# Four buffers for two exps, early tiles laid elsewhere, and a new order for two pairs of products and a few late jobs, in a fused attention and MLP kernel

## The chip, the cores and the metric

The kernel runs on one core of one Trainium2 chip. The metric is the device time of one execution in microseconds.

Engines in the profile: PE is the matmul engine (TensorE), PEld its weight loads, DVE is VectorE, ACT is ScalarE, POOL is GpSimd, SP issues most DMAs (25 of the 26 groups of DMA issues in the profile of the kernel before, ACT the other). "L1193" is a line of the kernel file; since the change adds lines, the same instruction has another line number after it.

## The reference

One input x of 2048 tokens by 1024 is layer-normalized and goes into two branches whose outputs are added to x.

```
xn = layernorm(x)
A: q, k, v = xn @ wq, xn @ wk, xn @ wv          # 32 heads of 32, four segments of 512 tokens
   per segment: p = softmax(q k^T * scale + causal mask);  a_dot = p v
                a_mem = phi(q) M / (phi(q) z)   # phi(t) = t + 1 if t > 0 else exp(t)
                o = g * a_mem + (1 - g) * a_dot
                M += phi(k)^T v;  z += sum phi(k)
   A = o @ wo
B: h = layernorm(xn);  u = gelu(h^T w1 + b1);  y = u w2 + b2;  B = y^T
out = x + A + B
```

## The kernel before

The kernel runs in three stages: the norm with the first ("early") 512 columns of w1; the MLP's products; attention in 32 units (four heads of one segment each).

**MLP products.** Each pair of 128-column blocks of w1 (and later of w2) is multiplied by a scheme of seven products instead of eight: products 1, 6, 5, 7, 2, 4, 3 of 8 (w1) or 14 (w2) matmuls of 128x512. They accumulate in three PSUM banks X, Y, Z; between two products on the same bank, DVE or ACT takes a partial sum out. Their operands are sums of w1 blocks ("sum") and differences of blocks of h or of the hidden layer g ("hT", "gT"; one of the gT is written over a g block), made on DVE.

```python
class _Pair:
    ACC = {1: "X", 2: "X", 6: "Y", 7: "Y", 4: "Y", 5: "Z", 3: "Z"}
...
# products():
order = [(0, 1), (1, 1), (0, 2), (1, 2)] + [(0, p) for p in (6, 5, 7, 4, 3)] + [(1, p) for p in (6, 5, 7, 4, 3)]
order += [(i, p) for i in range(2, n1 + self.N_W2) for p in self.ORDER]
...
# after1(), what follows product p of pair i:
elif p == 6:
    self.add_bank(pair, "Y", t2, t1)
    while self.later:                 # the g differences of pairs done, all at once
        self.later.popleft()()
...
elif p == 3:
    ...
    self.later.append(lambda: self.g_diff(j))        # four subtractions each
    if i == 0:
        self.later.append(lambda: self.g_diff(0))
        self.later.append(lambda: self.g_diff(1))
```

**Early tiles.** The input xin, a junk tile, a warm-up tile and the early w1 block lie where the hidden blocks g11, gT2, gT1, g12, g21, gT4, g22 come later, seven blocks of 14336 bytes a partition. In the kernel before, xin lies first and the early w1 block is under gT1 and g12. A gelu that writes g12 must therefore wait until the last matmul has read the early w1 block: in the trace one gelu runs at 31.45 us and the next seven from 34.47 us, with the early matmuls from 6.64 to 34.43 us.

**Attention.** For unit u, while its logits are exponentiated, the projections of unit u+2 run as fill-in jobs of 8 matmuls. The end of the q job puts three instructions on ACT and the end of the k job one on DVE and one on ACT:

```python
def q_job(self, u):
    def end(b):
        ... "act": qT[k] = copy of the bank
        if u >= N_GRP:
            ... "act": etmp[0] = exp(qT[k])          # writes etmp[0]
def k_job(self, u):
    def end(b):
        ... "dve": kT[k] = copy of the bank
        if u // N_GRP < N_SEG - 1:
            ... "act": etmp[1] = exp(kT[k])
def phi(self, dst, R_dst, src, R_src, k):           # k = 0 for q, 1 for k
    ... "dve": mtmp[k] = min(etmp[k], 1)            # reads etmp[k]
    ... "dve": dst = max(src + 1, mtmp[k])
def logits(self, u, step):                          # into banks 0 to 3
    ...
    ... "act": pT = exp(scale * banks 0..3)          # frees the banks for the next logits
```

Within unit u the program calls `logits(u, 0)`, `weigh(u-1, ..)`, `phi_k(u+1)`, `logits(u, 1)`, `combine(u-1)`, `phi_q(u+1)`, in even units `logits(u, 2)`, with fill-in matmuls between them. `combine` is about 3 us of DVE (476.53 to 479.37 us in one unit of the kernel before). The fill-in jobs also hold the products with wo of the segment before ("wo jobs"), each followed by an addition into fin on DVE.

The softmax here doesn't subtract the row's maximum and nothing guards it: scores larger than these inputs give would overflow.

Of the kernel before, what the change touches and what calls it, by code (L numbers as in the profile page):

```python
# [19 lines left out]
P = 128  # L20
# [364 lines left out]
class _Kernel:  # L385
# [33 lines left out]
    def alloc(self):  # L419
        k = _Walk(self.mem, 0, self.G_AT)  # L420

        def one(name, shape, dtype):
            t, (r,) = k.take(name, shape, dtype)
            setattr(self, name, t)
            setattr(self, "R_" + name, r)

        one("ident", [P, P], BF16)
        self.brow1, self.R_brow1 = k.take("brow1", [P, 32], BF16, 5)
        self.brow2, self.R_brow2 = k.take("brow2", [P, 32], BF16, 5)
        one("bcol", [P, 2, 32], BF16)  # L430
        one("b1c", [P, N_FCH], F32)
        one("b2c", [P, N_TCH], F32)
        one("beta", [P, N_HEAD], BF16)
        one("gcol", [P, N_HEAD], F32)
        one("gate", [P, N_GRP, 2, 4], F32)
        one("eps8", [P, 2, 4], F32)
        self.ln_st, self.R_st = k.take("ln_st", [P, N_TCH, 12], F32, N_TCH)
        self.ln_mv = k.take("ln_mv", [P, N_TCH, 2], F32)[0]
        self.ln_rs, self.R_rs = k.take("ln_rs", [P, N_TCH, 2], F32, N_TCH)
        self.R_rs0 = Res("rs0")  # L440
        one("expo", [P, N_TCH], F32)
        self.ln_sm = k.take("ln_sm", [P, N_TCH, 1], F32)[0]
        self.srec, self.R_srec = k.take("srec", [P, 2, 32], F32, 2)
        self.R_out = [Res(f"out{c}") for c in range(N_TCH)]

        e = _Walk(self.mem, self.G_AT, self.B_AT)
        self.xin, self.R_xin = e.take("xin", [P, N_TCH, D_MODEL], BF16, N_TCH)
        one_e = e.take("junk", [P, D_MODEL], BF16)
        self.junk, (self.R_junk,) = one_e
        self.warm, (self.R_warm,) = e.take("warm", [P, 512], BF16)  # L450
        self.w1early, self.R_w1e = e.take("w1early", [P, N_TCH, 512], BF16, N_TCH)

        b = _Walk(self.mem, self.B_AT + 6400, self.SB_END - self.SB_BASE)
        self.h = [[None, None], [None, None]]
        R = [[None, None], [None, None]]
        for k2 in range(2):
            both, res = b.take(f"h{k2}", [P, 2, 8, 512], F16, 1)
            self.mem.live.pop()
            for d in range(2):
                self.h[k2][d] = both[:, d]  # L460
                R[k2][d] = [Res(f"h{k2}{d}_{i}") for i in range(8)]
                lo = self.SB_BASE + b.at - 16384 + 8192 * d
                self.mem.live.append((lo, lo + 8192, R[k2][d]))
            setattr(self, f"h_{k2}", both)
        self.R_h = R
        self.hT, self.R_hT = [], []
        for i in (0, 1, 3):
            t, (r,) = b.take(f"hT{i}", [P, 8, 512], F16)
            self.hT.append(t[:])
            self.R_hT.append([r])  # L470
        self.hT.insert(2, self.h[0][1])
        self.R_hT.insert(2, R[0][1])
        self.w1s, self.R_w1s = [], []
        for i in range(2):
            t, (r,) = b.take(f"w1s{i}", [P, N_TCH, 256], BF16)
            self.w1s.append(t)
            self.R_w1s.append(r)
        self.s1, self.R_s1 = [], []
        for i in range(2):
            t, r = b.take(f"sum1_{i}", [P, 4, 8, P], F16, 4)  # L480
            self.s1.append(t)
            self.R_s1.append(r)
        self.tmp, self.R_tmp = [], []
        for i in range(6):
            t, (r,) = b.take(f"part{i}", [P, 512], F32)
            self.tmp.append(t)
            self.R_tmp.append(r)
# [214 lines left out]
    def products(self):  # L702
        fw = self.fw
        g = _Walk(self.mem, self.G_AT, self.B_AT)
        for b in range(8):
            if b == 0:
                self.alloc_hidden(g)
            self.gelu(b // 2, b % 2, self.bank(b), self.R_bank[b])
        self.h_diff((1, 2))
        self.pairs = {}  # L710
        n1 = self.N_W1
        order = [(0, 1), (1, 1), (0, 2), (1, 2)] + [(0, p) for p in (6, 5, 7, 4, 3)] + [(1, p) for p in (6, 5, 7, 4, 3)]
        order += [(i, p) for i in range(2, n1 + self.N_W2) for p in self.ORDER]
        self.later = deque()
        for i, p in order:
            if i not in self.pairs:
                self.begin_pair(i)
            pair = self.pairs[i]
            self.product(pair, p)
            pair.done.add(p)  # L720
            (self.after1 if i < n1 else self.after2)(pair, p)
# [22 lines left out]
    def h_diff(self, which):  # L744
        self.differences(self.h, self.R_h, self.hT, self.R_hT, which)

    def g_diff(self, j):
        self.differences([[t[:, j] for t in row] for row in self.gB], [[[r[j]] for r in row] for row in self.R_gB],
                         [t[:, j] for t in self.gT], [[r[j]] for r in self.R_gT], (1, 2, 3, 4))

    def begin_pair(self, i):
        n1 = self.N_W1
# [38 lines left out]
    def after1(self, pair, p):  # L791
# [13 lines left out]
                self.alloc_w2_first()  # L805
        elif p == 6:
            self.add_bank(pair, "Y", t2, t1)
            while self.later:
                self.later.popleft()()
        elif p == 7:  # L810
            self.add_bank(pair, "Y", t3, t1)
        elif p == 2:
            self.gelu(2 * j, 0, self.bank(pair.bank["X"]), self.R_bank[pair.bank["X"]])
        elif p == 4:
            if i + 2 < self.N_W1:
                self.w1_ring.ensure(i + 2)
            self.add_bank(pair, "Y", t1, t1)
            self.gelu(2 * j + 1, 0, self.tmp[t1][:], self.R_tmp[t1])
        elif p == 3:
            self.add_bank(pair, "Z", t2, t2)  # L820
            self.gelu(2 * j, 1, self.tmp[t2][:], self.R_tmp[t2])
            self.later.append(lambda: self.g_diff(j))
            if i == 0:
                self.later.append(lambda: self.g_diff(0))
                self.later.append(lambda: self.g_diff(1))
        if p in (5, 7) and {5, 7} <= d:
            self.add_bank(pair, "Z", t3, t3)
            self.gelu(2 * j + 1, 1, self.tmp[t3][:], self.R_tmp[t3])
# [11 lines left out]
                self.pair_sums(i + 1, (4,))  # L840
                self.alloc_w2_rest()
        elif i:
            if p == 7:
                self.pair_sums(i + 1, (1,))
            elif p == 2 and i > 1:
                self.pair_sums(i + 1, (2,))
            elif p == 4:
                self.pair_sums(i + 1, (2, 3) if i == 1 else (3,))
            elif p == 3:
                self.pair_sums(i + 1, (4,))  # L850
        elif p == 7:
            self.pair_sums(1, (1, 2))
        elif p == 3:
            self.pair_sums(1, (3, 4))

    W2_AT = (0, 14336)
    S2_AT = (38912 + 256, 53248 + 256)
# [132 lines left out]
    def before_attention(self, p):  # L990
# [23 lines left out]
        elif p == 5:  # L1014
# [4 lines left out]
                fw.op("pool", lambda e: e.memset(self.vA[k][:], 1.0), writes=self.R_vA[k])  # L1019
            self.qT, self.R_qT = many("qT", 3, [P, SEG_L], BF16)  # L1020
            self.kT, self.R_kT = many("kT", 3, [P, SEG_L], BF16)
            self.etmp, self.R_etmp = many("etmp", 2, [P, SEG_L], BF16)
            self.mtmp, self.R_mtmp = many("mtmp", 2, [P, SEG_L], BF16)
        elif p == 7:
            self.pqT, self.R_pqT = many("pqT", 3, [P, SEG_L], BF16)
# [32 lines left out]
                      reads=[self.R_diag], writes=[self.R_diag])  # L1058


    def phi(self, dst, R_dst, src, R_src, k):

        fw = self.fw
        et, mt = self.etmp[k], self.mtmp[k]
        fw.op("dve", lambda e: e.tensor_scalar(mt[:], et[:], 1.0, None, op0=ALU.min),  # L1065
              reads=[self.R_etmp[k]], writes=[self.R_mtmp[k]])
        fw.op("dve", lambda e: e.scalar_tensor_tensor(dst, src, 1.0, mt[:], op0=ALU.add, op1=ALU.max),  # L1067
              reads=[R_src, self.R_mtmp[k]], writes=[R_dst])

    def phi_q(self, u):  # L1070
        if N_GRP <= u < N_UNIT:
            k = u % 3
            self.phi(self.pqT[k][:], self.R_pqT[k], self.qT[k][:], self.R_qT[k], 0)

    def phi_k(self, u):
        if u // N_GRP < N_SEG - 1:
            k = u % 3
            self.phi(self.mtmp[1][:], self.R_mtmp[1], self.kT[k][:], self.R_kT[k], 1)

    def k_transpose(self, u):  # L1080
        if u // N_GRP < N_SEG - 1:
# [3 lines left out]
    def q_job(self, u):  # L1085
        def end(b):
# [1 line left out]
            fw.op("act", lambda e: e.activation(self.qT[k][:], self.bank(b), ACT.Copy),  # L1088
                  reads=[self.R_bank[b]], writes=[self.R_qT[k]])
            if u >= N_GRP:  # L1090
                fw.op("act", lambda e: e.activation(self.etmp[0][:], self.qT[k][:], ACT.Exp),  # L1091
                      reads=[self.R_qT[k]], writes=[self.R_etmp[0]])
        return self.proj_job(self.wq_ring, u, end)

    def k_job(self, u):
        def end(b):
# [1 line left out]
            fw.op("dve", lambda e: e.tensor_copy(self.kT[k][:], self.bank(b)),  # L1098
                  reads=[self.R_bank[b]], writes=[self.R_kT[k]])
            if u // N_GRP < N_SEG - 1:  # L1100
                fw.op("act", lambda e: e.activation(self.etmp[1][:], self.kT[k][:], ACT.Exp),
                      reads=[self.R_kT[k]], writes=[self.R_etmp[1]])
        return self.proj_job(self.wk_ring, u, end)

    def proj_job(self, ring, u, end):
# [208 lines left out]
    def attention(self):  # L1314
        self.jobs, self.turn = deque(), 0
        self.wo_plan = {}
        for s in range(N_SEG - 1):
            at = [N_GRP * s + 10 + n for n in range(8)] if s < 2 else [26, 27, 28, 29, 30, 30, 31, 31]
            for n, u in enumerate(at):
                self.wo_plan.setdefault(u, []).append((4 * s + n // 2, n % 2))  # L1320
        self.jobs.extend([self.q_job(0), self.k_job(0)] + [self.v_job(0, c) for c in range(4)])
# [59 lines left out]
    def tail(self):  # L1381
# [35 lines left out]
        product(4, 0, 7)  # L1417
        self.o_transpose(u, 4)
        product(3, 6, 7)
        for n in range(5):  # L1420
            product(n, 7, 8)
        for n in range(5, 7):
            product(n, 0, 8)
        product(7, 0, 8, ((0, 256), (256, 384), (384, 512)))


# [26 lines left out]
```

## Time and profile before

Three runs: 686.55, 684.60 and 682.38 us, median 684.6. The page of the profile, parts of its head (engine, busy us and share of the span, instructions):

```profile
span 682.0 us, 11096 instructions
PE 652.6 (96%) x4622; PEld 301.3 (44%) x4622; DVE 421.7 (62%) x789; ACT 282.8 (41%) x305; POOL 145.3 (21%) x181
```

TensorE is the limit, and only its idle stretches can be won without taking work away. The view of waits of PE (waiter, what it waited for: us in total, times, longest):

```profile
PE ps_all L198 <- ACT pT L1193: 16.2, 17, 1.8
PE ps_all L198 <- DVE part L688: 3.2, 2, 2.4
PE ps_all L198 <- DVE fin L1141: 1.9, 2, 1.3
```

The 3.2 us behind "part" are in the first two w1 pairs. The timeline of PE there (start us, us, engine, line, op, out<-in, tile, form, count; in brackets the idle time before it and what ended it):

```profile
34.27 1.89 PE L198 MATMUL ps_all<-h,w1s 128*128 128x512 f16 x8
36.46 1.89 PE L198 MATMUL ps_all<-h,w1s 128*128 128x512 f16 x8 [0.30 <-ACT g L740]
39.17 3.63 PE L198 MATMUL ps_all<-h,w1s 128*128 128x512 f16 x16 [0.83 <-ACT part L693]
48.76 1.90 PE L198 MATMUL ps_all<-hT,w1s 128*128 128x512 f16 x8 [0.78 <-DVE part L688]
...
59.96 3.54 PE L198 MATMUL ps_all<-hT,w1s 128*128 128x512 f16 x8 [2.39 <-DVE part L688]
63.34 1.89 PE L198 MATMUL ps_all<-h,sum 128*128 128x512 f16 x8
65.06 1.89 PE L198 MATMUL ps_all<-h,w1s 128*128 128x512 f16 x8
```

Two pairs are 14 products. A product of 8 matmuls that waits for nothing starts 1.73 us after the one before it, so 14 take 24.2 us; here 34.27 to 65.06 is 30.8 us. What the 2.39 us wait is made of shows in the timeline of DVE: twelve subtractions of gT and g, then the addition that the product at 59.96 waits for.

```profile
54.83 0.41 DVE L662 TENSOR_TENSOR gT<-g,g 128x512 f16<-128x512 f16 x1
...
58.89 0.42 DVE L662 TENSOR_TENSOR gT<-g,gT 128x512 f16<-128x512 f16 x1
59.22 1.41 DVE L688 TENSOR_TENSOR part<-ps_all,part 128x512 f32<-128x512 f32 x2
```

And 8 matmuls take 3.54 us after that gap instead of 1.89. The view of stretches of two us (stretch, its length, then busy us and count for PE, PEld, DVE, ACT and POOL; the granted clock, the DMA share, GB/s):

```profile
58.00:60.00 2.00, 0.04 (x1) 0.04 (x2) 1.93 (x6) 0.00 (x0) 0.00 (x0) 0.97 0.00 0
60.00:62.00 2.00, 2.00 (x5) 0.70 (x6) 1.23 (x2) 0.72 (x1) 0.00 (x0) 0.50 0.00 0
62.00:64.00 2.00, 2.00 (x8) 0.76 (x7) 0.46 (x1) 0.00 (x0) 0.00 (x0) 0.67 0.00 0
```

From 60 to 62 us PE is busy for 2.00 of 2.00 us, but with 5 matmuls at clock 0.50 (the view counts a matmul in every stretch that it touches): it is at half clock. So this stretch is 100% busy at half the rate, which only the count of matmuls and the clock column show.

The 16.2 us behind pT are in attention. One instance, the end of an even unit, in the timelines of ACT, then DVE, then PE:

```profile
478.54 0.60 ACT L1088 ACTIVATE qT<-ps_all 128x512 bf16<-128x512 f32 x1 [0.31 <-PE ps_all L198]
480.10 0.63 ACT L1091 ACTIVATE etmp<-qT 128x512 bf16<-128x512 bf16 x1 [0.96 <-DVE mtmp L1065]
480.64 1.86 ACT L1193 ACTIVATE pT<-ps_all 128x2048 bf16<-128x2048 f32 x1
...
479.29 0.72 DVE L1065 TENSOR_SCALAR mtmp<-etmp 128x512 bf16<-128x512 bf16 x1
...
482.55 0.40 PE L198 MATMUL ps_all<-qT,kT 32*128 32x512 bf16 x4 [1.02 <-ACT pT L1193]
```

The exp of q (L1091) can't overwrite etmp before phi of the unit before has read it (L1065, ended 480.01). The pT eviction stands behind it in ACT's queue, though its logits had been there since about 478.8, and the next logits on PE wait for that. ACT did not take the eviction out of turn: the trace has 0.96 us of ACT idle with the pT eviction ready behind. The view of waits of ACT in attention (370 to 682 us):

```profile
ACT etmp L1091 <- DVE mtmp L1065: 23.5, 16, 2.1
ACT etmp L1101 <- DVE kT L1098: 10.5, 14, 2.0
```

### The profile page before, as it was taken

The page shows a single profiled execution, that of the slowest core. Times are in us where ns is not written, and L with a number is a line of the kernel's source. Part 1 is how long each engine was busy: PE and PEld are TensorE (multiplying, and loading weights), DVE is VectorE, ACT ScalarE, POOL GpSimd, SP SyncE. Part 2 cuts the span into 40 slices and gives each one's busy share as a digit, 9 for nine tenths or more (in the row PEclk, how much of TensorE's full clock was granted, in tenths as well). Part 3 has the DMA queues.
Part 4 walks back from the last instruction along what each step waited for, and adds up shares of the span by engine and source line. Part 5 has one row for each costly group of instructions (what it writes and reads, how often), then busy time and mean ns, then how long its engine had stood idle before and what let it go on. Part 6 is the DMA issues. An engine that isn't in the chain of part 4 may idle for free.

```text
span 682.0 us, 11096 instructions
## 1 busy us (share of the span) xinstructions
PE 652.6 (96%) x4622; PEld 301.3 (44%) x4622; DVE 421.7 (62%) x789; ACT 282.8 (41%) x305; POOL 145.3 (21%) x181
## 2 busy tenths in 40 slices
PE   8988999999999999999999999998998899999888
PEld 3433444444444444444444444444444344444434
DVE  7857665656652445324531554697777897776685
ACT  7442132232300000000105878856666667666660
POOL 3500000000020122211240333322332232322240
PEclk9998999999999999999999999999999999999999
DMA  9704223242637654556385685665537755434314
GB/s 319 176 0 122 65 80 105 62 124 62 176 118 201 161 160 132 135 171 169 87 276 132 148 155 116 122 132 136 125 91 157 143 118 113 114 88 94 79 47 132
DMA packets 187242, 87.65 MB, mean 129 GB/s; under 512 B 116024, under 2 KB 174392, under 8 KB 187192
## 3 DMA queue, kind: packets, MB, share of 16 engines
q1 hardware_dynamic: 187048, 86.91, 51.0%
q8 instruction: 36, 0.59, 0.4%
q14 instruction: 14, 0.11, 0.1%
q10 hardware_dynamic: 144, 0.03, 0.0%
HBM read 67.13 MB, written 8.39 MB: 111 GB/s over the span
## 4 chain that ended last, share of the span: by engine, by line
PE 76%; DVE 13%; ACT 7%; DMA 3%; issue 1%; SPq 0%; ACTq 0%
PE ps_all L198 76%; ACT pT L1193 4%; DVE prod L1280 3%; DMA xs<-in_A_x_dram 2%; DVE mtmp L1065 2%; DVE o_s L1284 1%; ACT etmp L1091 1%; DVE ost L1243 1%; DVE mtmp L1067 1%; DVE fin L1141 1%; DVE srec L1278 1%; ACT g L740 1%; DMA xin<-in_A_x_dram 1%; DVE xs L981 1%; DVE srec L1279 0%
## 5 line engine op out<-in xcount | busy, mean ns | idle before, releaser
L1193 ACT ACTIVATE pT<-ps_all 128x2048 bf16<-128x2048 f32 x80 | 149.7, 1871 | 30.8 <-PE ps_all L198 30.7
L1197 POOL TENSOR_SCALAR_AFFINE_SELECT pT<-pT 128x512 bf16<-128x512 bf16 x128 | 92.2, 738 | 221.8 <-ACT pT L1193 221.8
L688 DVE TENSOR_TENSOR part<-ps_all,part 128x512 f32<-128x512 f32 x76 | 53.7, 706 | 124.8 <-PE ps_all L198 124.4
L921 POOL TENSOR_TENSOR part<-part,stg 128x512 f32<-128x512 f32 x24 | 33.0, 1404 | 269.3 <-DVE part L688 269.3
L693 ACT ACTIVATE part<-ps_all 128x512 f32<-128x512 f32 x20 | 11.9, 602 | 147.9 <-PE ps_all L198 147.9
L740 ACT ACTIVATE g<-part,b1c 128x512 f16<-128x512 f32 x36 | 26.0, 722 | 104.1 <-DVE part L688 104.1
L198 PE MATMUL ps_all<-wo,oT 128*128 128x512 bf16 (+2 forms) x272 | 64.7, 367 | 2.4 <-DVE fin L1141 1.9
L198 PE MATMUL ps_all<-wv,xnT 128*128 128x512 bf16 x256 | 66.6, 379 | 0.0
L198 PE MATMUL ps_all<-xnT,wq 128*128 128x512 bf16 x256 | 65.1, 380 | 0.0
L1243 DVE CAST ost<-ps_all 128x396 bf16<-128x396 f32 (+2 forms) x96 | 42.8, 473 | 34.6 <-PE ps_all L198 33.8
L198 PE MATMUL ps_all<-xnT,wk 128*128 128x512 bf16 x256 | 61.6, 380 | 0.0
L198 PE MATMUL ps_all<-g,w2s 128*128 128x512 f16 x224 | 51.0, 379 | 0.0
L198 PE MATMUL ps_all<-g,sum 128*128 128x512 f16 x224 | 51.0, 379 | 0.0
L198 PEld LDWEIGHTS ps_all<-vA,pT 128*128 128x128 bf16 x1280 | 42.2, 96 | 19.8 <-DVE ost L1243 10.2
L198 PE MATMUL ps_all<-gT,sum 128*128 128x512 f16 x224 | 49.7, 379 | 0.0
L198 PE MATMUL ps_all<-qT,kT 32*128 32x384 bf16 (+3 forms) x512 | 31.7, 301 | 16.5 <-ACT pT L1193 16.2
L198 PE MATMUL ps_all<-vA,pT 128*128 128x33 bf16 x1280 | 45.1, 178 | 1.6 <-DVE ost L1243 1.5
L198 PE MATMUL ps_all<-h,w1s 128*128 128x512 f16 x192 | 45.2, 379 | 1.1 <-ACT part L693 0.8
L198 PE MATMUL ps_all<-h,sum 128*128 128x512 f16 x192 | 45.4, 379 | 0.0
L198 PE MATMUL ps_all<-hT,sum 128*128 128x512 f16 x192 | 43.4, 379 | 0.0
L198 PEld LDWEIGHTS ps_all<-xnT,wk 128*128 128x128 bf16 x256 | 23.8, 98 | 29.8 <-issue 3.2
L198 PEld LDWEIGHTS ps_all<-wo,oT 128*128 128x128 bf16 x272 | 23.0, 97 | 28.6 <-issue 5.4
(98 smaller groups left out, 817.3 us busy)
## 6 DMA issues: line engine op xcount, KB each, us to landing
w2s<-in_B_w_dram SPq DMA_DIRECT2D x8, 1792.0 KB, 8.5
w1s<-in_B_w_dram SPq DMA_DIRECT2D x12, 1024.0 KB, 5.7
wq<-in_A_wq_dram SPq DMA_DIRECT2D x32, 256.0 KB, 3.4
wk<-in_A_wk_dram SPq DMA_DIRECT2D x32, 256.0 KB, 3.9
stg<-in_A_x_dram SPq DMA_DIRECT2D x16, 256.0 KB, 2.9
xs<-in_A_x_dram SPq DMA_DIRECT2D x16, 256.0 KB, 4.1
out_dram<-stg SPq DMA_DIRECT2D x16, 256.0 KB, 2.9
fin<-out_dram SPq DMA_DIRECT2D x16, 256.0 KB, 2.9
```

What stands on the lines that cost most here:

```text
L198: ins = self.nc.tensor.matmul(*args, **kwargs)
L688: self.fw.op("dve", lambda e: e.tensor_tensor(self.tmp[dst][:], self.bank(b), self.tmp[src][:], op=ALU.add), reads=[self.R_bank[b], self.R ...
L693: self.fw.op("act", lambda e: e.activation(self.tmp[dst][:], self.bank(b), ACT.Copy), reads=[self.R_bank[b]], writes=[self.R_tmp[dst]])
L740: self.fw.op("act", lambda e: e.activation(self.gB[f % 2][half][:, f // 2, :], src, ACT.Gelu_apprx_tanh, bias=self.b1c[:, f:f + 1], scale= ...
L921: fw.op("pool", lambda e: e.tensor_tensor(self.tmp[t][:], self.tmp[t][:], self.stg[k][:, 512 * half:512 * half + 512], op=ALU.add), reads= ...
L981: self.fw.op("dve", lambda e: e.tensor_scalar(x[:], x[:], self.ln_mv[:, c, 0:1], self.ln_rs[:, c, 0:1], op0=ALU.subtract, op1=ALU.mult), r ...
L1065: fw.op("dve", lambda e: e.tensor_scalar(mt[:], et[:], 1.0, None, op0=ALU.min), reads=[self.R_etmp[k]], writes=[self.R_mtmp[k]])
L1067: fw.op("dve", lambda e: e.scalar_tensor_tensor(dst, src, 1.0, mt[:], op0=ALU.add, op1=ALU.max), reads=[R_src, self.R_mtmp[k]], writes=[R_ ...
L1193: fw.op("act", lambda e: e.activation(dst, src, ACT.Exp, scale=SCALE), reads=self.R_bank[0:4], writes=[R[v % 2][kb] for v, kb, _ in blocks ...
L1197: fw.op("pool", lambda e: e.affine_select(d, d, pattern=[[0, 4], [1, P]], compare_op=ALU.is_ge, fill=0.0, base=0, channel_multiplier=-1), ...
L1243: fw.op("dve", lambda e: e.tensor_copy(dst, src), reads=[self.R_bank[b]], writes=[self.R_ost[o][part]])
L1280: fw.op("dve", lambda e: e.tensor_tensor(self.prod[:], ost[:, :, 0:D_HEAD], rec.unsqueeze(2).to_broadcast([P, 32, D_HEAD]), op=ALU.mult), ...
```

## The change

It is meant to take four kinds of idle time from PE: (1) lay the early tiles so that the first gelus need not wait for the last early matmul; (2) weave the products of the first two w1 pairs, and hand out the g subtractions one per product from pair 2 on; (3) give exp of q and exp of k a buffer for each parity of the unit; (4) at the end, move one wo job from unit 26 to unit 31 and one product of the tail ahead of the last pieces of the others.

```diff
-        self.xin, self.R_xin = e.take("xin", [P, N_TCH, D_MODEL], BF16, N_TCH)
         one_e = e.take("junk", [P, D_MODEL], BF16)
         self.warm, (self.R_warm,) = e.take("warm", [P, 512], BF16)
+        e.at = self.G_AT + 14336
         self.w1early, self.R_w1e = e.take("w1early", [P, N_TCH, 512], BF16, N_TCH)
+        e.at = self.G_AT + 3 * 14336
+        self.xin, self.R_xin = e.take("xin", [P, N_TCH, D_MODEL], BF16, N_TCH)
...
-        order = [(0, 1), (1, 1), (0, 2), (1, 2)] + [(0, p) for p in (6, 5, 7, 4, 3)] + [(1, p) for p in (6, 5, 7, 4, 3)]
+        order = [(0, 1), (1, 1), (0, 2), (1, 2), (0, 6), (0, 5), (0, 7), (1, 6), (0, 4), (1, 5), (1, 7), (0, 3), (1, 4), (1, 3)]
...
         elif p == 6:
             self.add_bank(pair, "Y", t2, t1)
-            while self.later:
-                self.later.popleft()()
...
-            self.later.append(lambda: self.g_diff(j))
-            if i == 0:
-                self.later.append(lambda: self.g_diff(0))
-                self.later.append(lambda: self.g_diff(1))
+            for jj in ((j, 0, 1) if i == 0 else (j,)):
+                for k in range(1, 5):
+                    self.later.append(lambda jj=jj, k=k: self.g_diff(jj, (k,)))
...   (the sums of w1 blocks for pairs 1 and 2 move to other products of pair 0)
+        if self.later and i > 1 and not (last and p == 3):
+            self.later.popleft()()
...
-            self.etmp, self.R_etmp = many("etmp", 2, [P, SEG_L], BF16)
+            self.etmp, self.R_etmp = many("etmp", 4, [P, SEG_L], BF16)
...   (exp of q of unit u: etmp[2 * (u % 2)]; exp of k: etmp[2 * (u % 2) + 1]; phi reads the same)
-            at = ... [26, 27, 28, 29, 30, 30, 31, 31]
+            at = ... [27, 28, 29, 30, 30, 31, 31, 31]
...   (tail)
-        for n in range(5):
+        product(5, 0, 7)
+        for n in range(6):
             product(n, 7, 8)
-        for n in range(5, 7):
-            product(n, 0, 8)
+        product(6, 0, 8)
```

More of the change, by code (lines that the diff above doesn't have):

```diff
@@ L745, in h_diff, with g_diff @@
         self.differences(self.h, self.R_h, self.hT, self.R_hT, which)
-    def g_diff(self, j):
+    def g_diff(self, j, which):
         self.differences([[t[:, j] for t in row] for row in self.gB], [[[r[j]] for r in row] for row in self.R_gB],
-                         [t[:, j] for t in self.gT], [[r[j]] for r in self.R_gT], (1, 2, 3, 4))
+                         [t[:, j] for t in self.gT], [[r[j]] for r in self.R_gT], which)
     def begin_pair(self, i):
@@ L842, in after1 @@
         elif i:
-            if p == 7:
+            if p == 7 and i > 1:
                 self.pair_sums(i + 1, (1,))
@@ L850, in after1 @@
                 self.pair_sums(i + 1, (4,))
-        elif p == 7:
+        elif p == 2:
             self.pair_sums(1, (1, 2))
+        elif p == 6:
+            self.pair_sums(1, (3,))
+        elif p == 5:
+            self.pair_sums(1, (4,))
         elif p == 3:
-            self.pair_sums(1, (3, 4))
+            self.pair_sums(2, (1,))
+        if self.later and i > 1 and not (last and p == 3):
+            self.later.popleft()()
     W2_AT = (0, 14336)
@@ L1058, in before_attention, with phi @@
                       reads=[self.R_diag], writes=[self.R_diag])
-    def phi(self, dst, R_dst, src, R_src, k):
+    def phi(self, dst, R_dst, src, R_src, k, u):
         fw = self.fw
-        et, mt = self.etmp[k], self.mtmp[k]
+        et, R_et, mt = self.etmp[2 * (u % 2) + k], self.R_etmp[2 * (u % 2) + k], self.mtmp[k]
         fw.op("dve", lambda e: e.tensor_scalar(mt[:], et[:], 1.0, None, op0=ALU.min),
-              reads=[self.R_etmp[k]], writes=[self.R_mtmp[k]])
+              reads=[R_et], writes=[self.R_mtmp[k]])
         fw.op("dve", lambda e: e.scalar_tensor_tensor(dst, src, 1.0, mt[:], op0=ALU.add, op1=ALU.max),
@@ L1072, in phi_q @@
             k = u % 3
-            self.phi(self.pqT[k][:], self.R_pqT[k], self.qT[k][:], self.R_qT[k], 0)
+            self.phi(self.pqT[k][:], self.R_pqT[k], self.qT[k][:], self.R_qT[k], 0, u)
     def phi_k(self, u):
@@ L1077, in phi_k @@
             k = u % 3
-            self.phi(self.mtmp[1][:], self.R_mtmp[1], self.kT[k][:], self.R_kT[k], 1)
+            self.phi(self.mtmp[1][:], self.R_mtmp[1], self.kT[k][:], self.R_kT[k], 1, u)
     def k_transpose(self, u):
@@ L1090, in end @@
             if u >= N_GRP:
-                fw.op("act", lambda e: e.activation(self.etmp[0][:], self.qT[k][:], ACT.Exp),
-                      reads=[self.R_qT[k]], writes=[self.R_etmp[0]])
+                fw.op("act", lambda e: e.activation(self.etmp[2 * (u % 2)][:], self.qT[k][:], ACT.Exp),
+                      reads=[self.R_qT[k]], writes=[self.R_etmp[2 * (u % 2)]])
         return self.proj_job(self.wq_ring, u, end)
@@ L1100, in end @@
             if u // N_GRP < N_SEG - 1:
-                fw.op("act", lambda e: e.activation(self.etmp[1][:], self.kT[k][:], ACT.Exp),
-                      reads=[self.R_kT[k]], writes=[self.R_etmp[1]])
+                fw.op("act", lambda e: e.activation(self.etmp[2 * (u % 2) + 1][:], self.kT[k][:], ACT.Exp),
+                      reads=[self.R_kT[k]], writes=[self.R_etmp[2 * (u % 2) + 1]])
         return self.proj_job(self.wk_ring, u, end)
@@ L1317, in attention @@
         for s in range(N_SEG - 1):
-            at = [N_GRP * s + 10 + n for n in range(8)] if s < 2 else [26, 27, 28, 29, 30, 30, 31, 31]
+            at = [N_GRP * s + 10 + n for n in range(8)] if s < 2 else [27, 28, 29, 30, 30, 31, 31, 31]
             for n, u in enumerate(at):
```

## The prediction

> **What bounds it now.** TensorE: the page has it busy 652.6 of 682.0 us (96%), and "in step" the matmuls start about 0.216 us apart (128x512; 590 in 129.15 us in the chain of waits). Only its idle stretches can be won. The view of waits (PE) adds them up: 16.2 us behind pT evictions (ACT, 17 times), 3.2 behind part additions (DVE), 1.9 behind fin additions.
>
> **1. First two w1 pairs (timeline, 34 to 65 us).** 14 products of 8 matmuls should take 14 x 1.728 = 24.2 us; they take 30.8 (34.27 to 65.06): 6.6 us lost. Idle: 0.30 and 0.83 us (gelu of early bank 1 started only at 34.47, after the last early matmul, because g12 overlays w1early), 0.78 (product (0,4) behind the addition of (0,7)), 2.39 (product (1,4) behind an addition queued after twelve gT/g subtractions of 0.42 us); each also costs about 0.15 us of refill. After the 2.39 us gap the granted clock was 0.50 for 2 us and 0.67 for the next 2, costing another 1.65 us. [...]
> The change lays g11/g12/g21/g22 over tiles whose readers are done, so gelus start bank by bank from 31.5; weaves the pairs so that a product on another bank lies between an addition and the next product on its bank; defers the subtractions to pairs 2 onward, one per product (56 x 0.42 us, DVE is only 58% busy there). Stepping through the new order with these durations I find no wait: **-6.4 us**.
>
> **2. Exp of q in attention.** ACT waits 23.5 us (16 times) to write etmp for q, because phi of the previous unit has not read it on a backlogged DVE; the next pT eviction, and then TensorE, wait behind it. Nine waits of TensorE show it (441 to 642 us: 1.28, 1.78, 1.02, 1.08, 1.78, 1.78, 1.02, 1.40, 1.70), 12.8 us, plus 0.15 each. With four buffers the exp waits for nothing but qT. What remains is ACT's qT copy, exp, pT in a row (0.6+0.6+1.8 us), about 0.25 us behind TensorE, as at 604.7 us (a pair of units there: 18.6 us, 18.5 busy). Exp of k still waits for the kT copy on DVE, so the small waits (0.22, one of 1.01 on ost) stay. DVE: busy about 16.7 of 19.4 us a pair, not the limit. **-11.9 us**.
>
> **3. End.** product(5,0..7) before the last oT covers the 0.47 us wait: **-0.6**. Moving one wo job from unit 26 to 31 fills unit 31, but the fin addition behind combine may hold the tail (0.69 us now): **+0.2**, at most 0.5 either way.
>
> Sum -18.7 us, all on the critical path: **about 666 us (662 to 670.5)**. Faster by over 2%: 0.90; within 2%: 0.095; slower: 0.005.
>
> **Right if:** (1,3) ends near 58.5 and the whole w2 part shifts by 6.4 us, granted clock 1.00 from 50 to 70; the ACT wait "etmp of q behind mtmp" vanishes and PE's wait for pT falls from 16.2 to 3-5 us; pairs of units 8 to 23 take 19.2-19.5 us instead of 20.3-21.2; TensorE busy time falls only by 1-2 us, its share to 98%.
>
> **Wrong if:** the faster pace makes DVE the limit (waits on ost, kT, mtmp grow), xs loads or transposes land late, or the deferred subtractions delay an addition in pairs 2 to 6; then attention keeps 4 to 6 us.

The clock of 0.50 and its 1.65 us are read from the profile of before, and the sum is -6.4 - 11.9 - 0.6 + 0.2 = -18.7 us. The 0.15 us of refill is that of the front: products start 2.19 us apart with a wait of 0.30 us between them (34.27 and 36.46) and 2.71 us apart with 0.83 us (36.46 and 39.17), where 1.73 us do without a wait. For the nine waits in attention it is the author's estimate, carried over from there, and was not shown: at the wait of 1.02 us above, the logits start 2.04 us after the wo matmuls before them (480.51 and 482.55), in the kernel after 1.12 us (472.25 and 473.37), so 0.92 us less.

## The result, and the profile after

After: 666.27, 667.62, 665.92 and 666.37 us, median 666.3. Before, on the same chip: median 685.6 of four runs. The ratio is 0.9729 (95% interval 0.9691 to 0.9768), 2.7% faster. All ratios here are the mean time of one kernel's fast runs over the mean of the other's in the same rounds, so not quite the ratio of the medians.

The page of the kernel after, the same lines:

```profile
span 664.5 us, 11075 instructions
PE 650.2 (98%) x4622; PEld 301.1 (45%) x4622; DVE 421.5 (63%) x789; ACT 282.9 (43%) x305; POOL 145.7 (22%) x181
```

No engine does less work: the counts of matmuls and of DVE and ACT instructions are the same. PE's busy time falls by 2.4 us; most of that is the half-clock stretch of before. Its waits:

```profile
PE ps_all L198 <- ACT pT L1198: 4.3, 11, 0.8
PE ps_all L198 <- DVE h L628: 1.8, 1, 1.8
PE ps_all L198 <- DVE ost L1248: 1.6, 3, 1.0
PE ps_all L198 <- DVE fin L1146: 1.3, 1, 1.3
```

The front, PE's timeline: no wait left, and 24.17 us from 35.26 to 59.43 for the 14 products.

```profile
35.26 7.07 PE L198 MATMUL ps_all<-h,w1s 128*128 128x512 f16 x32
...
57.70 1.89 PE L198 MATMUL ps_all<-h,sum 128*128 128x512 f16 x8
59.43 1.89 PE L198 MATMUL ps_all<-h,w1s 128*128 128x512 f16 x8
```

And the stretch that was at half clock:

```profile
60.00:62.00 2.00, 2.00 (x11) 0.88 (x9) 1.33 (x3) 1.32 (x2) 0.00 (x0) 1.00 1.16 330
```

In attention, the end of the same even unit, ACT then PE: the exp of q follows qT at once, and the logits come without a wait.

```profile
470.29 0.60 ACT L1093 ACTIVATE qT<-ps_all 128x512 bf16<-128x512 f32 x1 [0.32 <-PE ps_all L198]
470.92 0.63 ACT L1096 ACTIVATE etmp<-qT 128x512 bf16<-128x512 bf16 x1
471.46 1.86 ACT L1198 ACTIVATE pT<-ps_all 128x2048 bf16<-128x2048 f32 x1
...
473.37 0.40 PE L198 MATMUL ps_all<-qT,kT 32*128 32x512 bf16 x4
```

The waits of ACT in attention (370 to 665 us) have no line for exp of q any more, and a longer one for exp of k:

```profile
ACT etmp L1106 <- DVE kT L1103: 23.1, 16, 2.7
```

Of the 23.5 us that ACT spent waiting for phi of q, 12.6 (23.1 less 10.5) turned up again as a wait for the kT copy. The rest, 10.9 us, is close to what attention got shorter by; the traces do not tie the two together wait by wait. PE's waits show no loss from the longer wait of exp of k: those for pT are 4.3 us with it, against 16.2 before.

**Where the time went, stretch by stretch.** The starts of the first early matmul, the first w1 matmul and the first logits of units 0, 8, 25 and 29 in PE's timeline divide each span (the last column ends with the span):

```
kernel             first early  early part  w1 and w2, to unit 0  units 0-8  8-25    25-29  29 to end
before             6.64         27.63       334.99                62.14      173.32  36.91  40.37
after              7.45         27.81       328.18                61.53      163.94  34.14  41.45
exp buffers only   6.92         27.63       335.13                61.53      163.27  35.68  40.64
without them       6.83         29.29       328.24                61.53      173.33  35.36  41.52
exp of q only      6.97         27.70       328.23                62.52      163.24  34.14  41.60
old layout         7.07         29.31       329.61                62.18      163.23  34.14  41.46
old order          6.89         27.63       330.30                61.54      163.28  34.13  41.53
not deferred       6.45         29.32       332.15                61.92      163.25  34.14  41.47
after again        7.78         30.32       328.25                61.15      163.23  34.13  41.44
wo at 26           7.08         29.26       328.23                62.12      163.27  35.69  40.45
three wo in 30     6.74         27.77       328.24                62.11      163.25  34.14  41.15
combine last       7.14         27.62       329.54                62.11      163.25  34.13  40.01
fin first          6.84         28.13       328.26                61.15      163.27  34.13  39.72
12 warm-ups        7.01         27.83       328.19                62.11      163.27  34.13  39.76
```

Two things can be read here. First, a stretch that an edit does not touch repeats within 0.15 us from kernel to kernel from the third column on (units 0 to 8, which wait for a load of xs, within 1.4 us; "combine last" lost 0.2 and 0.8 us in two waits in the products that no other run shows; "after" lost 0.5 us in units 8 to 25, a wait behind a kT copy that had itself stood behind an xs load, DVE idle 1.18 us). So a stretch tells fractions of a microsecond that the times, which spread by 0.5 to 6 us within one kernel, do not. Second, what else varies lies mostly in the head: the first early matmul starts between 6.45 and 7.78 us, and the early part takes 27.6 to 28.1 or 29.3 to 30.3 us. (Each kernel has one profile; the spread of the other runs was not traced.)

The long early parts run at half the rate too. In the five kernels with 29.3 us or more, the first 8 to 13 early matmuls start 0.43 us apart instead of 0.216, which is 1.7 to 2.7 us more; in the other nine at most one gap is longer than 0.25 us. "After again", in stretches of one us (4 matmuls in each, then 6):

```profile
9.00:10.00 1.00, 1.00 (x4) 0.43 (x3) 1.00 (x4) 0.97 (x3) 0.40 (x1) 1.00 1.04 381
12.00:13.00 1.00, 1.00 (x4) 0.44 (x3) 0.86 (x4) 0.91 (x2) 0.55 (x1) 1.00 1.06 388
13.00:14.00 1.00, 1.00 (x6) 0.37 (x4) 1.00 (x3) 0.99 (x2) 0.40 (x1) 1.00 1.05 383
```

The clock column says 1.00 here. Of the five kernels it says 0.50 only in "old layout" (8 to 10 us, with 3 to 4 matmuls in each us); in the other four the half rate is read from the distance of the matmuls alone. It is not the edits that decide it: the same kernel has it in "after again" (30.32 us) and not in "after" (27.81 us).

The change from before to after is then +0.8 and +0.2 us in the head (chance), -6.8 in the products, -0.6 in units 0 to 8, -9.4 in units 8 to 25, and -1.7 in the rest, together -17.5 us, the difference of the spans.

### The profile page after: what moved, and what is told of

Read it like the earlier page. It is cut to its first block, busy times and chain, and to the rows that moved or that the text cites. A ratio compares the mean times of both kernels' runs of the same rounds, so it can differ in the third digit from the quotient of the medians.

```text
span 664.5 us, 11075 instructions
## 1 busy us (share of the span) xinstructions
PE 650.2 (98%) x4622; PEld 301.1 (45%) x4622; DVE 421.5 (63%) x789; ACT 282.9 (43%) x305; POOL 145.7 (22%) x181
## 4 chain that ended last, share of the span: by engine, by line
PE 81%; ACT 8%; DVE 7%; DMA 2%; issue 1%; SPq 0%; DVEq 0%
PE ps_all L198 81%; ACT pT L1198 6%; DMA xs<-in_A_x_dram 1%; DVE prod L1285 1%; ACT etmp L1096 1%; ACT qT L1093 1%; DVE mtmp L1070 1%; DMA xin<-in_A_x_dram 1%; DVE kT L1103 1%; DVE pqT L1072 1%; DVE o_s L1289 1%; ACT etmp L1106 1%; DVE fin L1406 1%; DVE ost L1248 0%; DVE xs L986 0%
```

## The experiments

Theory: the waits of PE add up. Front: layout about 1.4 us, order about 2, deferral the rest with the clock dip; attention: exp of q behind phi of q. Rivals: one part of the front carries it all; in attention exp of k matters as much, or the gain needs the other parts of the change.

**Exp buffers only** (kernel before, with the four buffers).

```diff
-            self.etmp, self.R_etmp = many("etmp", 2, [P, SEG_L], BF16)
+            self.etmp, self.R_etmp = many("etmp", 4, [P, SEG_L], BF16)
     (and the indices of the change)
```

> The kernel before with nothing changed but four exp buffers. My theory (exp of q waited for phi of the unit before, and the pT eviction and TensorE behind it): 11 to 12 us shorter than before, so ratio about 0.983; TensorE's waits for pT fall from 16.2 to about 4.5 us, ACT's waits of etmp of q for mtmp from 23.5 to 0, while the front still shows its 2.4 us gap. Rival (the gain in attention needs the earlier or smoother start, or the moved wo jobs): under 8 us.

Measured: median 673.9 us, ratio 0.9845 (0.9814 to 0.9875), 10.6 us by the ratio; the span fell by 11.2 us. The stretches from unit 8 on, where all nine long waits of before lie, give 11.0 us; units 0 to 8 give 0.6 more, within their scatter. PE's wait for pT:

```profile
PE ps_all L198 <- ACT pT L1193: 4.0, 10, 0.8
```

ACT's wait of etmp of q is gone, that of etmp of k went to 23.6 us (from 370 us on). The front is that of before, with 2.40 us of wait and granted clock 0.50 after it. The rival falls: the gain needs nothing else of the change.

**Without them** (kernel after, with two buffers).

```diff
-            self.etmp, self.R_etmp = many("etmp", 4, [P, SEG_L], BF16)
+            self.etmp, self.R_etmp = many("etmp", 2, [P, SEG_L], BF16)
     (and the indices of before)
```

> The kernel after with the exp buffers back to two. My theory: 11 to 12 us longer than after, so about 677.5 us, ratio to before about 0.990; nine waits of TensorE for pT of 1.0 to 1.8 us come back; products unchanged (no wait from 35 to 65 us). Rival (the wo move or the tail order had taken part of it): less than 9 us back.

Measured: median 679.6 us, ratio 0.9924. All nine waits came back with their sizes (1.02 to 1.79 us), and PE's wait for pT with them:

```profile
PE ps_all L198 <- ACT pT L1198: 16.2, 18, 1.8
```

In the stretches, units 8 to 25 take 173.33 against 163.25 us and units 25 to 29 take 1.22 us more: 11.3 us. The time is 12.4 us above that of "exp of q only" of the same rounds; the profile has 1.6 us more in its early part, the half rate at the head (matmuls 0.43 us apart).

**Exp of q only** (kernel after, with two buffers for q and one for k).

```diff
-        et, R_et, mt = self.etmp[2 * (u % 2) + k], self.R_etmp[2 * (u % 2) + k], self.mtmp[k]
+        j = 1 if k else 2 * (u % 2)
+        et, R_et, mt = self.etmp[j], self.R_etmp[j], self.mtmp[k]
...     (exp of k writes etmp[1] in every unit; etmp has 3 tiles)
```

> The kernel after with two buffers for exp of q and a single one for exp of k. My theory: only the q buffer was waited for (no wait of etmp of k for mtmp stands in the profile before), so the time of after, 666 us, within 1 us, ratio about 0.973. Rival (both exps block ACT, each half of the gain): 670 to 672 us, and a wait of etmp of k for mtmp shows up.

Measured: median 667.1 us, ratio 0.9747; units 8 to 25 take 163.24 us, as in after. No wait of exp of k for a phi appears. The fourth buffer is worth nothing here: phi of k runs early in the unit, long before the next exp of k (in before, which also has one buffer for k, phi's read of it ended at 475.55 and 487.67 us, and the next exp of k began at 482.40 and 493.17 us).

**Old layout** (kernel after, with the early tiles where they were).

```diff
+        self.xin, self.R_xin = e.take("xin", ...)      # first again
-        e.at = self.G_AT + 14336
-        e.at = self.G_AT + 3 * 14336
-        self.xin, self.R_xin = e.take("xin", ...)
```

> The kernel after with the early tiles laid as before (g12 over w1early). My theory: early bank 1's gelu waits again for the last early matmul, TensorE loses 0.46 and 0.98 us before products 2 and 3 of the w1 part, 1.4 us in all: about 667.8 us. Rival (the layout is what frees the whole front): 4 to 6 us longer, with waits also after 42 us.

Measured: 668.3 us. The waits of 0.30 us behind gelu and 0.82 us behind the copy are back, none later; the stretch of the products takes 329.61 instead of 328.2 us, 1.4 us, as expected.

**Old order** (kernel after, first two pairs in the old order with their sums at the old places, subtractions deferred).

```diff
-        order = [(0, 1), ..., (0, 6), (0, 5), (0, 7), (1, 6), (0, 4), (1, 5), (1, 7), (0, 3), (1, 4), (1, 3)]
+        order = [(0, 1), ...] + [(0, p) for p in (6, 5, 7, 4, 3)] + [(1, p) for p in (6, 5, 7, 4, 3)]
...   (the sums of w1 blocks for pairs 1 and 2 at their places of before)
```

> The kernel after with the first two w1 pairs in the old order and their weight sums at the old places; the g subtractions stay deferred to pair 2 and come one by one. My theory (12 queued subtractions made the 2.4 us gap and, with it, the clock dip; the order only hides one addition per pair): two waits of about 0.8 us, before (0,4) and before (1,4), no dip of the granted clock, so 1.9 us longer than after, about 668.3 us. Rival (the weave is what removes the gap): a wait over 2 us before (1,4) and the clock dip come back, 4 to 5 us longer.

Measured: 668.6 us. Two waits and no dip (granted clock 1.00 from 44 to 62 us); the stretch is 2.1 us longer than in after. PE's timeline:

```profile
47.56 1.90 PE L198 MATMUL ps_all<-hT,w1s 128*128 128x512 f16 x8 [0.79 <-DVE part L690]
...
57.16 1.90 PE L198 MATMUL ps_all<-hT,w1s 128*128 128x512 f16 x8 [0.79 <-DVE part L690]
```

The deferral alone thus turned the 2.39 us wait into one of 0.79; the weave takes away the two that are left.

**Not deferred** (kernel after, woven, subtractions all at once behind product 6).

```diff
         elif p == 6:
             self.add_bank(pair, "Y", t2, t1)
+            while self.later:
+                self.later.popleft()()
...
-        if self.later and i > 1 and not (last and p == 3):
-            self.later.popleft()()
```

> The kernel after, woven, but the g subtractions again all at once behind the addition after product 6 (now 16 of them at pair 2, as product (0,3) comes after (1,6)). My theory: the block of about 6 us on DVE only moves to pair 2; (2,4) then waits about 2.1 us for the addition of (2,7), and the granted clock dips or not: 2.3 to 4 us longer than after, 668.6 to 670.3 us. Rival (the weave alone was enough): within 1 us of after, no wait.

Measured: 669.1 us; the stretch is 4.0 us longer. PE's timeline and the stretches:

```profile
70.81 3.09 PE L198 MATMUL ps_all<-hT,w1s 128*128 128x512 f16 x8 [2.07 <-DVE part L690]
```

```profile
70.00:72.00 2.00, 1.19 (x5) 0.47 (x6) 1.97 (x4) 0.48 (x1) 0.00 (x0) 0.84 0.00 0
72.00:74.00 2.00, 2.00 (x6) 0.75 (x5) 0.83 (x3) 0.81 (x2) 0.00 (x0) 0.50 0.00 0
74.00:76.00 2.00, 2.00 (x9) 0.82 (x8) 1.23 (x2) 0.72 (x1) 0.00 (x0) 0.80 0.25 70
```

The block of subtractions has only moved to pair 2, sixteen of them now, and makes the same gap there with the same dip: 2.1 us of wait and about 1.9 of refill and half clock. Undoing layout, order or deferral alone costs 1.4, 2.1 and 4.0 us, 7.5 in sum, where all together gave 6.8: they overlap, most likely because the wait of product (1,4) is counted twice: it was one wait of 2.39 us before, and shows as 0.79 in "old order" and as 2.07 (there of product (2,4)) in this one. The 4.0 us are those of the profiled run, with its half clock; that may not come in every execution (point 4 below).

**Wo jobs at 26** (kernel after, wo jobs where they were), with **after again** in the same rounds.

```diff
-            at = ... [27, 28, 29, 30, 30, 31, 31, 31]
+            at = ... [26, 27, 28, 29, 30, 30, 31, 31]
```

> The kernel after, unchanged, for comparison on the same chip as the next three: 666 us (665 to 668). From the first logits on (363 us in the first profile) its stretches should repeat within 0.3 us, except for the one wait of 0.5 us behind a kT copy, which the other runs did not show; what varies should be the head, before the first early matmul and in the granted clock just after it.

> The kernel after with the wo jobs of the last segment back at 26, 27, 28, 29, 30, 30, 31, 31. The prediction gave the move +0.2 us; the two profiles suggest that it is worth about 0.4 us instead, since the wait of 0.69 us at the tail (fin addition behind combine) is gone and a wait of 0.27 for ost has come. So 0.3 to 0.6 us longer than after, from the stretches of the profile; the times alone may not tell it.

Measured: after again 665.5 us (ratio 0.9749), wo at 26 667.4 us (664.9 to 671.0; its ratio 0.9771, told "unclear"). The times can't tell them apart. The stretches from unit 25 on can: 76.14 us (35.69 + 40.45) against 75.57, so the move is worth 0.57 us (of which 0.18 is a wait for oT that only "wo at 26" shows). The tail's wait of 0.68 us is back:

```profile
648.84 1.47 PE L198 MATMUL ps_all<-wo,oT 128*128 128x512 bf16 x6 [0.68 <-DVE fin L1146]
```

With the wo jobs and the tail's order both old ("exp buffers only") the same stretches take 76.32 us, 0.18 us more, hardly above their scatter. From the last transposes to the end of the span the order of the tail shows better: 9.69 and 9.70 us in the two kernels with the old order, 9.42 to 9.45 in the twelve with the new one. It is worth 0.26 us. After again also had an early part of 30.32 us in its profile with nothing changed.

**Three wo jobs in unit 30**, then **combine last**, **fin first** and **12 warm-up matmuls**: what is left after the change is mostly one wait of 1.27 us at the start of unit 31, behind a fin addition that stands on DVE behind combine(29) and phi_q(31). These four build on each other; the diffs are against after.

```diff
-            at = ... [27, 28, 29, 30, 30, 31, 31, 31]
+            at = ... [27, 28, 29, 30, 30, 30, 31, 31]       # three wo in 30
...
-            if u:
+            if u and u < N_UNIT - 1:                        # combine last ("fin first": u < N_UNIT - 2)
                 self.combine(u - 1)
-            self.phi_q(u + 1)
+            if u != N_UNIT - 2:                             # fin first
+                self.phi_q(u + 1)
...
                 self.dense(cuts[3])
+                if u == N_UNIT - 2:                         # fin first
+                    self.combine(u - 1)
                 self.logits(u, 2)
             self.dense(100)
+            if u == N_UNIT - 2:                             # fin first
+                self.phi_q(u + 1)
+        self.combine(N_UNIT - 2)                            # combine last
         self.tail()
...
-    N_WARM = 10
+    N_WARM = 12                                             # 12 warm-up matmuls
```

> The kernel after with the moved wo jobs at units 27, 28, 29, 30, 30, 30, 31, 31 rather than 27, 28, 29, 30, 30, 31, 31, 31: one job more in unit 30, whose first job then ends ahead of the combine on DVE. If the waits of unit 30 (0.58 for pT, 1.27 behind the fin addition queued after combine and phi) come from too few matmuls between the logits, both nearly go, 1.8 us; the wait of 0.7 us at the tail behind the last fin addition comes back. Net 0.5 to 1.2 us shorter than after.

Measured: 665.4 us; from unit 29 to the end 41.15 us against 41.45, 0.3 us, less than expected: of the two waits in unit 30 the one of 0.58 us went, but 1.19 of the 1.27 us stayed, and the tail's 0.69 us came back. One of the three jobs of unit 30 now ends ahead of combine (its addition runs at 632.84 us), but the next two additions still stand behind combine and phi_q, at 637.57 us, and PE waits for the first of them.

> As the run before it, and in unit 31 the combine of unit 30 is issued after the last wo jobs, so that their fin additions no longer stand behind it on DVE. If the tail's 0.7 us wait is that queue, it goes, and the time is 1.3 to 2 us shorter than after, unless the combine, some 1.5 us later, delays the transpose of its o and with it the products of the tail that read it (then 0 to 1 us longer).

Measured: 665.3 us; that stretch takes 40.01 us, 1.4 us less than in after and 1.1 less than with three wo in 30 alone, and the tail's wait is gone: the additions no longer stand behind combine.

> As the run with combine last, and in unit 30 too the combine and the phi of q come after the fin additions that they delayed. If the wait of 1.19 us at the start of unit 31 is that DVE queue, it goes: the stretch from the first logits of unit 29 to the end, 41.45 us in after and 40.0 with combine last, takes about 38.7 us, and the time is 2.5 to 3 us shorter than after (ratio to after about 0.996). Rival (the tail then waits for the later transposes of o): 39.5 us or more.

Measured: 663.8 us (663.25 to 664.73, four runs), the lowest of all kernels, ratio to before 0.9720; the mean is 663.9 against 665.9 us for after again of the same rounds (0.997). The stretch takes 39.72 us, not the 38.7 that were expected. The 1.19 us wait went, but phi_q(31) now stands ahead of the take-out of unit 30's sums, and a new wait came:

```profile
640.27 0.57 PE L198 MATMUL ps_all<-vA,pT 128*128 128x33 bf16 x16 [0.88 <-DVE ost L1248]
```

The number is that of the rival (39.5 or more), but the transposes were not waited for, so the rival is not the reason. Most of the wait moved to another DVE instruction of the same full queue.

> As the run before it, with 12 instead of 10 warm-up matmuls, which end at about 6.4 us, just before the first early matmul (6.5 to 7.5 us in the profiles so far). If the spread of some 2 us in the head is the granted clock falling in that gap, the early part takes 27.8 us and never 29.4, and the mean is 0.5 us below that of the run before it with a smaller spread. If it is only the landing of the first loads: no change within 0.3 us.

Measured: 664.3 us (664.01 to 664.50, four runs), mean 664.3 against 663.9: no gain. The spread is the smallest of all (0.5 us, where the run before it has 1.5), and the early part of its one profile takes 27.83 us, at full rate (6 or 7 matmuls in nearly every us), but so it was in eight of the 13 profiles with ten warm-up matmuls; four runs and one profile don't show that the warm-up did it. That stays open.

## Why the prediction was right or wrong, point by point

The prediction said 666 us; the median is 666.3. Its large terms held, its small ones did not. That the sum came so near is in part luck: the errors of the terms below partly cancel, and the head alone moves a run by more than 0.3 us.

1. **Front, predicted -6.4 us: -6.8** in the stretch of the products. No wait is left, and the granted clock is 1.00. The single experiments give the parts: layout 1.4, order 2.1, deferral 4.0 us with the clock. "(1,3) ends near 58.5" came out as 59.4, because the first early matmul started 0.8 us later and the early part took 0.2 us more; neither belongs to the change. For the same reason the w2 part shifts by 5.8 and not by 6.4 us in this pair of profiles.
2. **Exp of q, predicted -11.9 us: -11.0 to -11.3** by the stretches from unit 8 on of the two experiments that add and remove it, and -10.6 by the time of the first, whose interval (8.6 to 12.7) holds the prediction. PE's wait for pT fell to 4.3 us (3 to 5 was said). Pairs of units took 19.1 to 19.5 us but for one with 20.2. The waits that were said to stay (0.22, and 1.01 on ost) stayed at those sizes. Not foreseen: that about half of ACT's wait would turn up again as a longer wait of exp of k for the kT copy.
3. **End, predicted -0.6 (tail) and +0.2 us (wo job): -0.26 and -0.57.** Both terms were wrong, one in sign; the sums, -0.4 and -0.8, lie near each other by luck. For the moved wo job, the step that failed is that the fin addition behind combine holds the tail. In the timeline of before, combine starts behind the fin addition of the unit's first wo job. With three jobs in unit 31 that job ends sooner, its addition runs at 640.7 us, ahead of the ost copies, combine ends 2.0 us after the start of the last logits instead of 3.3, and the 22 matmuls of wo jobs that follow them run without a wait. For the tail, the step that failed is that what PE wins there shortens the kernel. PE did win it: its last matmul ends 6.73 us after the transposes instead of 7.38, 0.65 us. But the last addition ends only 0.51 us sooner (7.20 for 7.71), because the last ten additions, 0.6 us for a full one, now come in a row, and DVE is busy without a pause from 657.3 to 662.3 us. The span then ends 2.23 us after that addition instead of 1.99; why was not tested. DVE now ends the chain of waits of after:

```profile
655.33 2.60 PE ps_all L198 x12
658.52 3.60 DVE fin L1406 x7
```

4. The clock step held in the profiles: a wait of 2.07 to 2.40 us was followed by a granted clock of 0.50 in each of the three kernels that had one (before, exp buffers only, not deferred), and 2.1 us of idle in the head of "old layout" by 0.50 from 7.5 to 10.9 us. The waits of 1.78 and 1.79 us in attention, and all shorter ones after the head, were not: the clock is 1.00 around each of them. But this is one profile for each kernel. Of the 25 other executions of before in the rounds of the experiments, 13 report a mean granted clock of 1.00 and take 682.7 us on average, the other 12 take 685.5; of the four of "not deferred" the two with 1.00 take 668.3, the others 670.1. A single stretch of 3.4 us at half clock (59.9 to 63.3 us in the profile of before) would make the mean 0.9975. So the half clock may be missing from about half of the executions, and the front then be worth some 1.7 us less; since the clock column also said 1.00 while the matmuls started 0.43 us apart in the head of "after again", this stays open.

## What to carry to other kernels

When an engine works through its queue in order, as ACT did here (0.96 us idle with the pT eviction ready), and writes a small scratch tile, ask who read it last: a single spare buffer (here the one for exp of q, not the one for exp of k) freed what stood behind it in the queue, 11.0 to 11.3 us. Hand out bulk work on a helper engine one piece at a time between the urgent pieces, since a block of it turned up as one gap here, and a gap of 2.07 us on the matmul engine came with a loss of 4.0 us in the profiled run of "not deferred". Judge edits worth under 1 us by the stretches of the trace between fixed points, which repeated within 0.15 us where the early part alone varied by 2.7 us (27.6 to 30.3), and at the end of a kernel check the helper's queue as well before booking a removed wait as won.
